# First queries in two column parts, weight chunks between the early loads, and new lengths in a planner: a fused attention and max-out kernel

## The chip, the cores and the metric

The kernel runs on one core of a Trainium2 chip. The time is device microseconds for one launch; before the change it is 384.32 us, the median of three runs (384.29 to 386.53). The profile is of one execution whose span is 382.8 us. Lines such as L436 are lines of the kernel before.

The engines are called PE (matrix multiply), ACT (scalar engine), DVE (vector engine), POOL (GpSimd) and SP (the engine that issues the DMAs here).

## The reference

There are 8 batches of 8 heads, 1152 positions and head size 64. Queries are averaged in pairs of positions, so that 576 remain; attention follows; the heads are put side by side into x (4608 tokens by 512), and a max-out layer ends it.

```python
q_pool = q.reshape(B, H, S // 2, 2, D).mean(axis=3)
scores = scale * np.matmul(q_pool, k.transpose(0, 1, 3, 2))
attn = softmax(scores)
x = (attn @ v), heads side by side           # 4608 x 512
g = np.maximum(x @ w1, x @ w2)               # 4608 x 1024
out = g @ w_out                              # 4608 x 512
```

## The kernel before, in words

**Tiling.** Work goes by pairs of heads, 32 in all, four to a batch. A pair's scores are 9 key tiles by 576 queries for each head. They are laid end to end in one row and cut into groups of 512 columns (`W`), 324 groups in all, so a pair is 10.125 groups. A group is two or more matmuls of 64 rows, both heads beside each other on the two halves of the array (L429), into one of three score buffers; one ACT instruction takes the exp of 128x1024 values (L436) into `et`. When all groups of a pair have been through exp, PE multiplies them with the values (L378), ten units of nine matmuls, and DVE divides by the row sums (L388, L390) into `xnat`.

**Before the scores.** Keys and values are cast to bf16 on POOL (L273, L304), queries are added in pairs on POOL (L297). Both are transposed, for the first five pairs on PE with a copy by DVE (L323, L349, L330, L356), later by DMA. Pair 0 is different: its two query halves, one a head and 64 partitions wide, are loaded by two DMAs (L258) and added by DVE; its keys are cast by ACT in two pieces (L279).

**The max-out layer.** It uses max(a, b) = b + max(a - b, 0). The weights come in twelve chunks: four of w2, four of w_out, four of w1. DVE casts them; `wd` is w1 - w2 (L519); w2 is transposed on PE (L531) and multiplied by w_out once into `w21` (L547, 32 matmuls of 512 columns). The work for tokens is then `h` jobs (x times `wd`, L582, and a maximum with zero, L593) and `p` jobs (x times `w21` plus the maximum times w_out, L609, twelve matmuls for 128 tokens, one copy out of PSUM by L620 or L623, and two stores by L567). It can begin when all four pairs of batch 0 are through attention and transposed into `xT`, and `wd` is there.

**The planner.** Python code writes the order out when the kernel is built. `Plan` keeps a clock for each engine and adds a `cost` in us for each operation; an engine executes its list in that order and waits on semaphores, so a wrong cost changes no result, but puts work behind a wait that the planner did not foresee. The main loop picks what PE does next: a burst of score groups if their buffers and inputs are due (`burst_now`), or a unit of one of two jobs in hand (`lane`). `burst_size` says how many groups a burst has: three if the finished batches hold over 600 tokens that the last layer has not done, else two. In the planner each change between 64-row and 128-row matmuls costs PE 0.1 us.

**Loads.** A fixed list at the end says in which order the early loads go to SP after those of pair 0, keys and queries of pair 1 and values of pair 0: k2, q2, the four w2 chunks, v1, k3, q3, the four w_out chunks, v2, k4, q4, v3, the four w1 chunks. Loads of later pairs are appended when a buffer has been read.

**The end.** The last `p` job is like the others: twelve matmuls of 512 columns, one copy by DVE, two stores issued one after the other by SP.

The lines that matter most:

```python
                    r=[f"s{r}"], w=keys + [f"s{r}"], cost=0.24 + (z - a) / 700.0)   # L438, exp
            return 3 if len(done) * SQ - p_end[0] > LAG else 2                     # L772
```

Of the kernel before, what the change touches and what calls it, by code (L numbers as in the profile page):

```python
# [15 lines left out]
class Plan:  # L16
# [38 lines left out]
    def op(self, eng, fn, r=(), w=(), dma=None, cost=0.1, mode="f", after=(), solo=False):  # L55
        n = len(self.ops)
        assert all(k in self.writer for k in r), r
        deps, raw = self.deps(r, w, after)
        prev = self.last.get(eng)
        if prev is not None and (solo or self.ops[prev]["solo"]):  # L60
            deps.add(prev)
            raw.add(prev)
        self.last[eng] = n
        t = self.when(eng, r, w, after)
        if dma is not None:
            self.free[eng] = t + (1.3 if mode == "t" else 0.5)
            self.dma_free = max(self.free[eng] + 1.2, self.dma_free) + cost
            seen = self.dma_free + 0.7
        else:
            if eng == "PE" and mode != self.mode:  # L70
                t += 0.1
                self.mode = mode
            self.free[eng] = t + cost
            seen = t + cost + self.LAT[eng]
        self.ops.append(dict(eng=eng, fn=fn, deps=deps, raw=raw, dma=dma, w=tuple(w),
                             seen=seen, end=self.free[eng], solo=solo))
        for k in r:
            self.readers.setdefault(k, set()).add(n)
        for k in w:
            self.writer[k] = n  # L80
            self.readers[k] = set()
        return n
# [71 lines left out]
def bass_funnel_attn__then__act_maxout2_kernel(  # L154
# [32 lines left out]
    with ctx:  # L187
# [10 lines left out]
        qp = [sbuf([HP, QU, 2, D], BF16, f"qp{s}") for s in range(2)]  # L198
# [31 lines left out]

        def setup():
# [21 lines left out]
        def load_q(i):  # L253
            b, h0, s = i // NHP, 2 * (i % NHP), i % 3
            for half in range(2) if i == 0 else (None,):
                at = slice(0, P) if half is None else rows(half)
                hs = slice(h0, h0 + 2) if half is None else slice(h0 + half, h0 + half + 1)
                op("SP", lambda e, at=at, hs=hs: e.dma_start(  # L258
                    qraw[s][at, :, :, :].rearrange("p u r d -> p (u r d)"),
                    q[b, hs, :, :].rearrange("h (p r) d -> (h p) (r d)", p=HP)),  # L260
                    w=["qraw0.0"] if half == 0 else [f"qraw{s}"],
                    dma="d_q" if half == 0 else f"d_q{s}", cost=1.45 if half is None else 0.75)
# [8 lines left out]
        def cast_k(i):  # L271
# [4 lines left out]
                w=[f"kbf{s}"] + (["kbf0.0", "kbf0.3"] if i == 2 else []), cost=1.13)  # L276
# [15 lines left out]

        def cast_q(i):
            s, r = i % 2, i % 3
            for half in range(2):
                a = qraw[r][rows(half), :, :, :]
                op("DVE" if i == 0 else "POOL", lambda g, half=half, a=a: g.tensor_tensor(  # L297
                    qp[s][:, :, half, :], a[:, :, 0, :], a[:, :, 1, :], ALU.add),
                    r=["qraw0.0" if i == 0 and half == 0 else f"qraw{r}"], w=[f"qp{s}.{half}"], cost=0.65 if i == 0 else 1.4,
                    solo=i > 0 and half == 1)  # L300
# [16 lines left out]
        def qtrans(i):  # L317
# [10 lines left out]
            def evac(m):  # L328
                mb = fb[m][:, :].bitcast(BF16)
                dve(lambda e: e.tensor_copy(qpT[i % 3][:, :], mb[:, 0:SQ]),  # L330
                    [f"f{m}"], [f"qpT{i % 3}", f"f{m}"], 0.4)
            return Job("q", [unit([f"qp{s}.0", f"qp{s}.1", "ident"], 0.3, go, "s")], evac, ("q", i))

# [7 lines left out]
        def ktrans_pe(i, cuts=(0, 5, 9)):  # L341
# [3 lines left out]
            for lo, hi in zip(cuts, cuts[1:]):  # L345
# [8 lines left out]
                def evac(m, lo=lo, hi=hi):  # L354
# [4 lines left out]
                        [f"f{m}"], kkeys(i, lo, hi) + [f"f{m}"], 0.1 + (hi - lo) * 0.12)  # L359
# [5 lines left out]
        def av_jobs(i):  # L365
# [5 lines left out]
            need = [f"et{es}.{g - first(i)}" for g in range(first(i), after(i))] + [f"vE{vs}", "pad"]  # L371

            def chunk(half, sb):
# [8 lines left out]
                return unit(need, 0.275, go)  # L382
# [37 lines left out]
        def skeys(g):  # L420
            return [key for i, t, *_ in pieces(g) for key in (f"kT{i % 3}.{t}", f"qpT{i % 3}")]

        def scores(g):
# [10 lines left out]
            def exp(a, z, keys):  # L434
# [3 lines left out]
                    r=[f"s{r}"], w=keys + [f"s{r}"], cost=0.24 + (z - a) / 700.0)  # L438
# [20 lines left out]
        def under(n0, n1):  # L459

            keys = [key for key, lo, hi in (("w2b", 512, 1536), ("w2T", 1536, 2560),
                                            ("w2f", 2560, NTOK)) if n0 < hi and lo < n1]
            if "w2T" in keys:
                keys += [f"w2T{ct}" for ct in range(NC_)]
            return keys
# [48 lines left out]
        def w_cast(part, ct):  # L514
            if part == 0:
                dve(lambda e: e.tensor_copy(w2b[:, ct, :], w2f[:, ct, :]),
                    [f"w2f{ct}"], [f"w2b{ct}", "w2b"], 0.6)
            elif part == 1:
                dve(lambda e: e.tensor_tensor(  # L519
                    wd[:, ct, :], w1f[:, ct, :], w2f[:, ct, :], ALU.subtract),  # L520
                    [f"w1f{ct}", f"w2f{ct}"], [f"wd{ct}", "w2f"], 1.2)
            else:
                dve(lambda e: e.tensor_copy(  # L523
                    wo[:, 2 * ct:2 * ct + 2, :], wof[:, 2 * ct:2 * ct + 2, :]),
                    [f"wof{ct}"], [f"wo{2 * ct}", f"wo{2 * ct + 1}"], 0.6)

        def w2t_job(ct):
# [7 lines left out]
            def evac(m):  # L535
# [3 lines left out]
                    [f"f{m}"], [f"w2T{ct}", "w2T", f"f{m}"], 1.15)  # L539
            return Job("w", [unit([f"w2b{ct}", "w2b", "ident"], 0.44, go)], evac)  # L540
# [19 lines left out]
        def store(lo, s):  # L560

            for half in range(2):
                n0 = lo + half * HP
                b, at = n0 // SQ, n0 % SQ
                if b % 2:
                    at = (at - NB) % SQ
                op("SP", lambda e, b=b, u=at // HP, half=half: e.dma_start(  # L567
                    out[b * SQ:(b + 1) * SQ, :].rearrange("(p u) e -> u p e", u=QU)[u, :, :],
                    osb[s][rows(half), :]), r=[f"osb{s}"], dma=f"d_o{s}", cost=0.4)
# [4 lines left out]
        def h_jobs(nb, tail):  # L574
# [4 lines left out]
            for ft in range(NF):  # L579
# [6 lines left out]
                def evac(m, ft=ft):  # L586
# [5 lines left out]
                    else:  # L592
                        dve(lambda e: e.tensor_scalar_max(  # L593
                            gT[:, ft, g0:g0 + size], fb[m][:, 0:size], 0.0),
                            [f"f{m}"], w, 0.1 + size / 960.0)
# [3 lines left out]
        def p_job(lo, tail):  # L599
            hi = lo + P  # L600

            def part(j):
                def go(e, m):
# [5 lines left out]
                    return e.matmul(fb[m][:, :], lhs, rhs, start=(j == 0), stop=(j == NC_ + NF - 1))  # L609
                if j < NC_:  # L610
                    return unit([f"w21{j}"] + xkeys(lo, hi), 0.216, go)
                return unit([f"wo{j - NC_}", f"gT.{lo % RING // P}.{j - NC_}"], 0.216, go)

            def evac(m):
                o = ocount[0] % 4
# [6 lines left out]
                else:  # L622
                    dve(lambda e: e.tensor_copy(osb[o][:, :], fb[m][:, :]),  # L623
                        [f"f{m}"], [f"osb{o}", f"f{m}"], 0.63)
                held[o] = (lo, o)
            return Job("p", [part(j) for j in range(NC_ + NF)], evac, nb=hi)
# [65 lines left out]

        def start_w(n):
            for ct in range(NC_):
                load("w", (n, ct), got_w, f"{('w2f', 'w1f', 'wof')[n]}{ct}")
# [73 lines left out]
        def burst_size():  # L769

            done = [b for b in range(B) if all(av_half.get(b * NHP + j) == 2 for j in range(NHP))]
            return 3 if len(done) * SQ - p_end[0] > LAG else 2  # L772

        def more_moe():
# [10 lines left out]
            while p_at[0] + P <= h_end[0] and f"w21{NC_ - 1}" in plan.writer:  # L785
                queue["p"].append(p_job(p_at[0], tail))
# [58 lines left out]
        def emit_unit(kk):  # L845
# [21 lines left out]
            if job.done:  # L867
# [7 lines left out]

        setup()
# [3 lines left out]
        cast_k0(0, 3, "kraw0.0")  # L880
        cast_q(0)
        cast_k0(3, NT, "kraw0")
        queue["q"].append(qtrans(0))
        queue["k"].extend(ktrans_pe(0, (0, 3, NT)))
        load_k(1)
        load_q(1)
# [6 lines left out]
        load("k", 2, load_k, "kraw2")  # L893
        load("q", 2, load_q, "qraw2")
        start_w(0)
        load("v", 1, load_v, "vraw1")
        load("k", 3, load_k, "kraw0")
        load("q", 3, load_q, "qraw0")
        start_w(2)
        load("v", 2, load_v, "vraw2")  # L900
        load("k", 4, load_k, "kraw1")
        load("q", 4, load_q, "qraw1")
        load("v", 3, load_v, "vraw0")
        start_w(1)
# [46 lines left out]
        def _(sp):  # L951
            plan.emit("SP", sp, sem, last_waits=[f"d_o{s}" for s in range(4)])
# [40 lines left out]
```

The softmax here doesn't subtract the row's maximum and nothing guards it: scores larger than these inputs give would overflow.

## Time and profile before

| what | value |
|---|---|
| time, median of 3 | 384.32 us |
| span of the profiled execution | 382.8 us |
| PE busy | 363.7 us (95%) |
| ACT busy | 316.9 us (83%), of it exp 307.8 |
| POOL busy | 162.0 us (42%) |
| DVE busy | 140.2 us (37%) |
| first score matmul; first exp | 8.27 us; 8.91 us |
| first matmul of w21; first of an h job | 43.59 us; 65.85 us |
| last copy out of PSUM begins | 378.72 us |

Busy time of PE is modelled and runs on into the next matmul, so how much PE could still do is read better from the starts of its matmuls than from its share. Shares are means over quite different stages: the first 60 us with their loads, some 270 us in which exp and matmuls go on side by side, and about 50 us at the end in which PE works alone.

### The profile page before, as it was taken

Reading aid. Unit: us, or ns where it says so; the run is one execution under the profiler, and the core shown is the slowest. Engines: PE = TensorE matmul, PEld = TensorE weight load, DVE = VectorE, ACT = ScalarE, POOL = GpSimd, SP = SyncE. Lnnn points to the kernel's source line nnn. Section 1 sums busy time; section 2 is a strip of 40 time slices with the busy share of each in tenths; the row PEclk is TensorE's granted clock in tenths of the full one; section 3 lists DMA queues with packets and bytes.
Section 4 is the critical chain, followed back from the end, with each engine's and each line's share of the span. In section 5 each row is a group of like instructions: output and inputs, shape, how many; then the busy total and the mean of one; then the engine's idle time right before and its main releaser. Section 6 shows DMA issues by size and latency. Waiting matters only on the chain.

```text
span 382.8 us, 11318 instructions
## 1 busy us (share of the span) xinstructions
PE 363.7 (95%) x5010; PEld 210.8 (55%) x5010; DVE 140.2 (37%) x283; ACT 316.9 (83%) x355; POOL 162.0 (42%) x135
## 2 busy tenths in 40 slices
PE   2787999999999999999999999999999999999995
PEld 1365546555555555455556565555455655667642
DVE  2274934442234223422252224422442244237201
ACT  3998989999999999999999999999899999902210
POOL 1955597665554555555453535545545110000000
PEclk9999999999999999999999999999999999999999
DMA  8999999999989998999799999999899460121144
GB/s 248 405 391 399 392 257 312 331 309 312 225 234 295 273 272 174 309 320 275 142 265 289 319 179 212 286 258 315 200 236 267 94 109 14 29 44 42 29 95 98
DMA packets 93521, 88.58 MB, mean 231 GB/s; under 512 B 66080, under 2 KB 66592, under 8 KB 93472
## 3 DMA queue, kind: packets, MB, share of 16 engines
q1 hardware_dynamic: 93472, 87.86, 89.4%
q8 instruction: 39, 0.64, 0.7%
q14 instruction: 10, 0.08, 0.1%
HBM read 62.91 MB, written 9.44 MB: 189 GB/s over the span
## 4 chain that ended last, share of the span: by engine, by line
PE 85%; DMA 6%; DVE 4%; POOL 2%; issue 1%; SPq 1%; POOLq 0%
PE fb L378 22%; PE fb L609 21%; PE sps L429 18%; PE fb L582 15%; PE sps L609 4%; DMA qraw<-in_q_dram 3%; DMA kraw<-in_k_dram 2%; PE sps L582 2%; DVE wd L519 2%; POOL qp L297 1%; PE fb L547 1%; DVE xnat L390 1%; POOL vE L304 1%; PE fb L489 1%; DVE wo L523 1%
## 5 line engine op out<-in xcount | busy, mean ns | idle before, releaser
L436 ACT ACTIVATE et<-sps 128x1024 bf16<-128x1024 f32 (+1 forms) x336 | 307.8, 1005 | 19.0 <-PE sps L429 17.2
L378 PEld LDWEIGHTS fb<-vE,et 128*128 128x128 bf16 x2880 | 93.4, 97 | 20.9 <-issue 10.9
L378 PE MATMUL fb<-vE,et 128*128 128x65 bf16 x2880 | 101.9, 193 | 0.3
L297 POOL TENSOR_TENSOR qp<-qraw 64x576 bf16<-64x576 f32 x62 | 88.6, 1429 | 30.6 <-DMA qpT<-qp 21.3
L429 PE MATMUL sps<-qpT,kT 64*128 64x512 bf16 (+7 forms) x1152 | 96.9, 289 | 3.0 <-ACT et L436 2.1
L304 POOL TENSOR_SCALAR vE<-vraw 128x1152 bf16<-128x1152 f32 x32 | 36.9, 1152 | 103.2 <-PE fb L378 95.8
L429 PEld LDWEIGHTS sps<-qpT,kT 64*128 64x128 bf16 x1152 | 41.8, 95 | 51.3 <-issue 19.6
L582 PE MATMUL fb<-xT,wd 128*128 128x512 bf16 (+3 forms) x276 | 63.1, 360 | 0.7 <-DVE stage L623 0.7
L609 PE MATMUL fb<-wo,stage 128*128 128x512 bf16 x240 | 62.4, 380 | 0.0
L593 DVE TENSOR_SCALAR stage<-fb 128x512 bf16<-128x512 f32 (+3 forms) x64 | 41.9, 657 | 32.3 <-PE fb L582 32.1
L388 DVE RECIPROCAL rc<-fb 128x5 f32<-128x5 f32 x64 | 12.4, 194 | 112.3 <-PE fb L378 112.3
L273 POOL TENSOR_SCALAR kbf<-kraw 128x1152 bf16<-128x1152 f32 x31 | 36.2, 1167 | 14.6 <-DMA kraw<-in_k_dram 12.5
L582 PEld LDWEIGHTS fb<-xT,wd 128*128 128x128 bf16 x276 | 22.8, 98 | 29.4 <-DVE stage L593 6.3
L623 DVE COPY stage<-fb 128x512 f32<-128x512 f32 x29 | 20.0, 690 | 50.2 <-PE fb L609 49.7
L609 PEld LDWEIGHTS fb<-wo,stage 128*128 128x128 bf16 x240 | 21.1, 97 | 23.3 <-issue 3.3
L390 DVE TENSOR_TENSOR xnat<-fb,rc 128x320 bf16<-128x320 f32 x64 | 31.5, 491 | 2.2
L609 PE MATMUL fb<-w,xT 128*128 128x512 bf16 x120 | 32.1, 380 | 0.0
L609 PEld LDWEIGHTS fb<-w,xT 128*128 128x128 bf16 x120 | 10.3, 98 | 11.7 <-issue 2.0
L589 ACT ACTIVATE stage<-sps 128x256 bf16<-128x256 f32 (+1 forms) x7 | 2.3, 338 | 16.4 <-PE sps L582 16.4
L620 ACT COPY stage<-sps 128x512 f32<-128x512 f32 x3 | 1.8, 585 | 13.8 <-PE sps L609 13.8
L609 PE MATMUL sps<-wo,stage 128*128 128x512 bf16 x48 | 11.3, 379 | 0.0
L582 PE MATMUL sps<-xT,wd 128*128 128x256 bf16 (+2 forms) x76 | 10.3, 275 | 0.0
(40 smaller groups left out, 96.4 us busy)
## 6 DMA issues: line engine op xcount, KB each, us to landing
vraw<-in_v_dram SPq DMA_DIRECT2D x32, 576.0 KB, 7.7
kraw<-in_k_dram SPq DMA_DIRECT2D x31, 576.0 KB, 6.6
qraw<-in_q_dram SPq DMA_DIRECT2D x31, 576.0 KB, 5.8
out_dram<-stage SPq DMA_DIRECT2D x72, 128.0 KB, 2.4
xT<-in_moe_w_dram SPq DMA_DIRECT2D x4, 512.0 KB, 11.9
stage<-in_moe_w_out_dram SPq DMA_DIRECT2D x4, 512.0 KB, 14.2
stage<-in_moe_w_dram SPq DMA_DIRECT2D x4, 512.0 KB, 13.2
qraw<-in_q_dram SPq DMA_DIRECT2D x2, 288.0 KB, 4.1
```

The lines of the kernel that those rows point to most:

```text
L273: op("POOL", lambda g: g.tensor_scalar(kbf[s][:, :, :, :].rearrange("p t h d -> p h t d"), kraw[r][:, :, :, :], 1.0, 1.0, ALU.mult, ALU.mu ...
L297: op("DVE" if i == 0 else "POOL", lambda g, half=half, a=a: g.tensor_tensor(qp[s][:, :, half, :], a[:, :, 0, :], a[:, :, 1, :], ALU.add), ...
L304: op("POOL", lambda g: g.tensor_scalar(vE[r][:, :, :, 0:D].rearrange("p t h d -> p h t d"), vraw[r][:, :, :, :], 1.0, 1.0, ALU.mult, ALU.m ...
L378: last = e.matmul(fb[m][:, sb * 66:sb * 66 + 65], et[:, a:a + P], vE[vs][:, t, half, 0:65], start=(t == 0), stop=(t == NT - 1))
L388: dve(lambda e: e.reciprocal(rc[half][:, :], a[:, :, 64:65]), [f"f{m}"], [f"rc{half}"], 0.19)
L390: dve(lambda e: e.tensor_tensor(xnat[xs][:, :, c:c + D], a[:, :, 0:D], rc[half][:, :].unsqueeze(2).to_broadcast([P, NCH + 1, D]), ALU.mult ...
L429: last = e.matmul(sps[r][:, h, col:col + hi - lo], kT[i % 3][rows(h), t, :], qpT[i % 3][rows(h), lo:hi], start=True, stop=True)
L436: op("ACT", lambda e: e.activation(et2[:, :, c:c + z - a], sps[r][:, :, a - g * W:z - g * W], EXP, scale=scale), r=[f"s{r}"], w=keys + [f" ...
L582: return e.matmul(fb[m][:, 0:size], wd[:, ct, ft * P:(ft + 1) * P], xT[:, ct, n0:n1], start=(ct == 0), stop=(ct == NC_ - 1))
L593: dve(lambda e: e.tensor_scalar_max(gT[:, ft, g0:g0 + size], fb[m][:, 0:size], 0.0), [f"f{m}"], w, 0.1 + size / 960.0)
L609: return e.matmul(fb[m][:, :], lhs, rhs, start=(j == 0), stop=(j == NC_ + NF - 1))
L623: dve(lambda e: e.tensor_copy(osb[o][:, :], fb[m][:, :]), [f"f{m}"], [f"osb{o}", f"f{m}"], 0.63)
```

## The change

It has five parts.

1. **The first queries.** The pair-0 load is cut by columns (five and four of nine) and not by heads, so each part covers all 128 partitions. DVE adds each part on 128 partitions (`cast_q0`), and PE transposes it in 64x64 blocks (`qtrans0`). The first keys are cast, transposed and copied in three pieces (1, 2 and 6 tiles), not two (3 and 6), so that the first score group can begin with one key tile.
2. **The order of early loads.** q1 goes ahead of k1; the weight chunks (a: w2, b: w_out, c: w1) are spread singly between the loads of queries, keys and values.
3. **The planner's lengths.** exp goes from 0.24 + n/700 to 0.05 + n/600 (0.971 to 0.903 us for a full group); DVE copies and maxima get 0.16 us in place of 0.1 or so; the first DMA starts at 0.78 us, not at 0. `burst_size` gives three as soon as any batch is finished.
4. **Waits.** Weight keys are kept by chunk, so a transpose of one w2 chunk no longer waits for the cast of a later one. The last value unit of a pair, which reads 64 columns past its own scores, now names the neighbour's first group as an input.
5. **The last tile.** It is two jobs, 384 and 128 columns. ACT empties the first while PE does the second; DVE empties the second, whose stores go out from SP and ACT, one each.

```diff
+            if not self.dma_free:
+                t = 0.78
...
+        Q0 = (0, 5, QU)
...
-            for half in range(2) if i == 0 else (None,):
+            for lo, hi in zip(Q0, Q0[1:]) if i == 0 else ((0, QU),):
...
+        def cast_q0(j):
+            lo, hi = Q0[j:j + 2]
+            op("DVE", lambda e: e.tensor_tensor(
+                q0[:, lo:hi, :], qraw[0][:, lo:hi, 0, :], qraw[0][:, lo:hi, 1, :], ALU.add),
+                r=["qraw0" if j else "qraw0.0"], w=[f"qp0.{j}"], cost=0.1 + (hi - lo) * 0.07)
...
+                past = [f"et{1 - es}.0"] if sb == NCH and not es & half else []
+                return unit(need + past, 0.275, go)
...
-                    r=[f"s{r}"], w=keys + [f"s{r}"], cost=0.24 + (z - a) / 700.0)
+                    r=[f"s{r}"], w=keys + [f"s{r}"], cost=0.05 + (z - a) / 600.0)
...
-            return Job("w", [unit([f"w2b{ct}", "w2b", "ident"], 0.44, go)], evac)
+            return Job("w", [unit([f"w2b{ct}", "ident"], 0.44, go)], evac)
...
+                if c0 == 0:
+                    op("ACT", lambda e: e.copy(osb[o][:, c0:c1], fb[m][:, 0:c1 - c0]),
+                       r=[f"f{m}"], w=[f"osb{o}", f"f{m}"], cost=0.16 + (c1 - c0) / 1200.0)
+                    store(lo, o, c0, c1)
+                else:
+                    dve(lambda e: e.tensor_copy(osb[o][:, c0:c1], fb[m][:, 0:c1 - c0]),
+                        [f"f{m}"], [f"osb{o}", f"f{m}"], 0.16 + (c1 - c0) / 960.0)
+                    store(lo, o, c0, c1, ("SP", "ACT"))
...
-            return 3 if len(done) * SQ - p_end[0] > LAG else 2
+            return 3 if done else 2
...
-                queue["p"].append(p_job(p_at[0], tail))
+                if p_at[0] + P < NTOK:
+                    queue["p"].append(p_job(p_at[0], tail))
+                else:
+                    queue["p"].extend(p_job(p_at[0], tail, *c) for c in ((0, 384), (384, E)))
...
+        K0 = (0, 1, 3, NT)
...
+        for lo, hi in zip(K0, K0[1:]):
+            cast_k0(lo, hi, "kraw0.0" if hi <= 3 else "kraw0")
+        queue["k"].extend(ktrans_pe(0, K0))
+        load_q(1)
         load_k(1)
-        load_q(1)
...
-        start_w(1)
+        whole = {"q": load_q, "k": load_k, "v": load_v}
+        part = {"a": (0, "w2f"), "b": (2, "wof"), "c": (1, "w1f")}
+        for kind, i in zip(*[iter("q2a0a2k2a1a3b1b0b2v1b3c0v2k3q3k4q4c2c1v3c3")] * 2):
```

## The prediction

> **What bounds the kernel.** I read the page's slices first, then the stages.
>
> ```profile
> PE   2787999999999999999999999999999999999995
> ACT  3998989999999999999999999999899999902210
> ...
> DMA  8999999999989998999799999999899460121144
> ```
>
> A slice is 9.57 us. PE is full from the fifth slice to the end, ACT until 332 us only, DMA is full at the start. So from 40 us on the kernel ends when PE's list ends; ACT has some 47 us to spare. Only four things can move the end: PE's idle time before it is full, PE's own overhead later, waits that a new order brings, and what follows the last matmul.
>
> ```profile
> 0.00:8.00 8.00, 1.09 (x12) 0.74 (x12) 2.09 (x4) 2.35 (x3) 0.97 (x10) 1.00 0.76 217
> 8.00:12.00 4.00, 3.62 (x28) 1.86 (x29) 0.77 (x2) 3.39 (x5) 2.36 (x2) 1.00 1.04 400
> ...
> 20.00:30.00 10.00, 8.95 (x180) 6.67 (x179) 7.57 (x14) 9.97 (x13) 5.16 (x4) 1.00 1.05 391
> 30.00:40.00 10.00, 7.48 (x159) 5.08 (x157) 4.51 (x10) 8.96 (x11) 6.25 (x5) 1.00 1.04 402
> 40.00:60.00 20.00, 18.94 (x280) 10.63 (x276) 12.89 (x20) 18.95 (x22) 15.85 (x11) 1.00 1.13 321
> 60.00:80.00 20.00, 19.92 (x307) 11.57 (x306) 8.97 (x19) 19.82 (x23) 13.88 (x12) 1.00 1.13 314
> ```
>
> The third number is PE's busy time. Idle is 6.91 in the first 8 us, 2.44 from 8 to 20 (the rows left out give 0.90 and 1.16), and 1.05 + 2.52 + 1.06 = 4.63 from 20 to 60. Then 0.08.
>
> ```profile
> PE fb L323 <- DVE qp L297: 6.7, 1, 6.7
> PE sps L429 <- ACT et L436: 2.1, 5, 0.5
> PE fb L349 <- POOL kbf L273: 1.5, 1, 1.5
> ```
>
> PE's waits (total, count, longest): the start hangs on the first queries. PE hardly waits for exp. The 1.5 us is at 35.25: the transpose of k4, whose load landed at 33.98 by its semaphore, blocks PE, and ACT stands 1.03 us.
>
> **What the Trainium skill says.** SBUF — State Buffer, section Door 1: partitions 0 to 63 reach 8 of the 16 DMA ports, 196 GB/s against 328 for 128 partitions at 1 MiB. The trace agrees: in slices of 1.5 us the DMAs moved
>
> ```profile
> GB/s 0 123 258 259 377 415 398 393 407 410 412 407 400 394 406 385 387 392 382 388 394 413 386 405 406 410 397 413 392 392 404 319 129 356 392 438 203 108 229 369
> ```
>
> 258 while the query halves were on their way, some 400 later. TensorEngine Tiling, Key Properties: a change of tiling mode drains the array; the trace prices it below. DMA: Bandwidth & Descriptors, "Issuing engines are not separate DMA queues": a second issuing engine saves only issue time; no run here shows two yet.
>
> **Part 1, start.** DVE gets the first half at 4.61 and the second at 5.91 (starts of its adds), the key pieces land at 6.42 and 7.44. ACT casts 7.46 to 8.30, the first exp is at 8.91. The queries' 590 KB at 390 GB/s take 1.5 us; from 2.0, where packets begin, to 4.5 they took 2.5. I let all later landings come 1.0 us earlier, up to 1.4 if the slow first packets go too: keys at 5.4 and 6.4. The adds are 0.75 for 576 elements; with 1.04 ns an element (DVE copies of 128 and 512 columns: 0.29 and 0.69) they are 0.48 and 0.42, hidden before the keys. The 18 blocks are no longer than the 9 transposes (0.66) by more than 0.3, also before the keys. One key tile then goes through cast 0.31, transpose 0.2, copy 0.23 and gaps in 1.2 us, against 1.85 for three, so the first score would be at 6.6. But ACT has the cast of six tiles (0.84) in its list before the first exp: 6.4 + 0.84 + 0.1 = 7.35. Gain 8.91 - 7.4 = **1.5 us** (0.8 to 1.8). Exp paces the next 20 us, so all moves with it.
>
> **Part 2, load order.** A 576 KB load takes 1.45 us, a chunk 1.31 (differences of landings: 9.30, 10.72, 12.24; 15.18 to 21.80 for four chunks and v1). From keys at 6.4 the new list lands: q1 7.9, k1 9.3, v0 10.8, q2 12.2, w2 chunks 13.6 to 18.9, w_out chunks 20.2 to 25.6 (before: about 26.9 to 31), v1 24.3, c0 26.9, v2 28.4, k3 29.8, q3 31.3, k4 32.7, q4 34.2, last w1 chunk 39.5 (42.1). The product w21 needs all of w2 and w_out: possible from 27.5, before it began at 43.59:
>
> ```profile
> 43.59 1.25 PE L547 MATMUL fb<-wo,xT 128*128 128x512 bf16 x5
> ...
> 65.85 1.03 PE L582 MATMUL fb<-xT,wd 128*128 128x512 bf16 x4
> ```
>
> It is 32 x 0.216 = 6.9 us of PE work, in exactly the stretch where PE idles 4.6 us. Before, it came after that stretch, held both lanes, and delayed the value products of pair 3 (exp done at about 46, last unit at 57.8) and with it the first h job. Balance: a pair costs PE 10.1 groups at 0.31 with switches, 90 value matmuls at 29.5 ns (2.65) and 1.1 of transposes, 6.9 in the 9.27 us that exp takes. From 27.5 the w21 work fills the rest until about 48, then x of batch 0 is ready at some 52 and h begins at 52 to 57. Idle from 20 to 60 falls from 4.6 to 0.8: **3.8 us** (1.5 to 4.6). Queued behind the late k3 and q3: q3 lands at 31.3, POOL adds for 2.9, transpose and copy 1.1, ready at 35.3; pair 3 needs it at 7.4 + 30.4 x 0.92 = 35.4. A near miss; that is the 0.8 I leave. If it is late, the scores queued on PE stand, and exp behind them.
>
> **Part 3, lengths and bursts.** Back-to-back exps start 0.903 us apart in the trace, which is what the new formula says; the old 0.971 was long. So bursts come no earlier than the buffers do; I add no wait. Switches:
>
> ```profile
> 94.25 1.51 PE fb L609 x7
> 96.52 2.27 PE fb L609 x10
> 98.79 0.76 PE sps L429 x12
> ```
>
> In the chain, seven matmuls take 7 x 0.216 = 1.51; ten after a switch 2.27 - 2.16 = 0.11 more; three groups 0.76 - 0.65 = 0.11 more. Start to start it is 0.095 each way, 0.19 a burst. Counting runs of L429 after 60 us: 107 bursts for 271 groups, 65 of three groups, 36 of two. All in threes would be 91: 16 x 0.19 = 3.0. Some twos come from inputs and not from the rule; I take 11: **2.1 us** (0.5 to 3.0). Longer bursts let ACT stand a little; it has 47 us.
>
> **Part 4, waits.** Dropped chunk waits: in the shadow of DVE's lazy casts, 0. The new input of the last value unit: seven pairs in eight share that group with the next pair and wait for it anyway; behind it queue the unit's lane and a later exp. 0 to 0.3 in all.
>
> **Part 5, end.** Last matmul ends 378.70, copy 0.69, SP issues at 379.44 and 379.95, landed 382.33. After: 12 x (162 + 56) ns is as long as 12 x 216. The 128-column copy takes 0.29 (row above), saving 0.40. But SP first issues two stores of the 384 part: ACT's copy 0.585 - 128 x 0.83 = 0.48 ends 0.2 before the last matmul, so SP is free 1.0 after it; its third issue starts 0.25 earlier than the last one before, with a quarter of the bytes. **0.4 us** (0.1 to 0.8).
>
> Sum: 1.5 + 3.8 + 2.1 + 0.4 = 7.8, less 0.1 for part 4: 384.3 - 7.7 = 376.6.
>
> **Rivals.**
> - *The loads take it back.* q3 and v2 come 6 us later than before (q3 landed at 25.5). If DMA runs 1 to 2 us behind my table, PE stands behind pair 3 as it did behind k4, and idle from 20 to 60 stays at 4 us. For: the 0.1 us margin. Against: w21 can be put before it. 1.5 + 0.6 + 1.0 + 0.3: 380.9.
> - *PE waits for exp.* With an exact exp length every burst is due at the last moment, and any lag makes PE stand with h and p work queued behind it. Before, the slack was 3 x 0.07 a burst and waits were 2.1 us. At 0.1 for 110 bursts that is 11 us, against gains of 7.7: 387.6, slower. Against: PE's value units are planned at 0.275 and take 0.266, so PE, too, has little lead, and the pitch is exact.
> - *All of it.* Bursts all of three, no idle after 20, start 1.8: 1.8 + 4.6 + 3.0 + 0.8 = 10.2: 374.1 or a little under.
>
> **Numbers.** Mine 0.62, all of it 0.14, loads 0.15, PE waits 0.09. The range 373 to 381.5 holds the first two and most of the third. Below 380.5 are the first two and a few of the third: 0.78; within 1% 0.14; slower 0.08.
>
> **What would show it.** First exp near 7.4; L547 from about 28 and L582 from 52 to 57; PE idle from 20 to 60 under 1.5; L429 runs after 60 us near 96; PE waiting for L436 still around 2 us; SP's last issue 1.0 after the last matmul. I am wrong if PE's waits for exp pass 5 us, if ACT stands over 2 us near 35, or if h begins no earlier.

## The result and the profile after

The changed kernel takes 390.64 us, the median of four runs (388.70 to 392.97), against 384.81 us for the kernel before, also the median of four: ratio 1.0147, 95% interval 1.0102 to 1.0192. It was to be faster by 2%, and is slower by 1.5%. The profiled execution, the fastest of the four, has a span of 386.9 us, against 382.8. The time lies some 1.8 us above the span in every run.

The slices of the page, PE and ACT:

```profile
PE   3898989999999999999999999999999999999994
ACT  3998989999999999999999999999999985111121
```

PE is as full as before, to the end. ACT's row falls off one to two slices earlier: exp is done at 324.0 us, 11.1 before its old end, and PE does not end earlier for it. The stages that the prediction costed, with the same columns (the third number is PE's busy time):

```profile
0.00:8.00 8.00, 2.10 (x23) 0.97 (x23) 1.96 (x6) 2.24 (x4) 0.97 (x10) 1.00 0.74 252
8.00:12.00 4.00, 2.88 (x24) 1.34 (x26) 0.56 (x1) 3.46 (x5) 1.37 (x2) 1.00 1.02 405
...
20.00:30.00 10.00, 9.06 (x194) 6.79 (x192) 6.17 (x12) 9.93 (x13) 1.48 (x3) 1.00 1.05 393
30.00:40.00 10.00, 8.36 (x155) 5.58 (x150) 7.03 (x14) 8.94 (x11) 9.49 (x7) 1.00 1.03 403
40.00:60.00 20.00, 17.41 (x271) 9.79 (x268) 13.27 (x16) 18.63 (x22) 18.54 (x13) 1.00 1.07 310
60.00:80.00 20.00, 19.97 (x301) 11.79 (x300) 9.39 (x20) 18.95 (x23) 12.13 (x10) 1.00 1.15 293
```

Idle from 20 to 60 us is 0.94 + 1.64 + 2.59 = 5.2 us; it was 4.6 and was to be 0.8. From 40 to 60 it rose from 1.06 to 2.59. POOL is fuller there (18.54 for 15.85). In the first 12 us PE works 4.98 us, before 4.71. So the start gave next to nothing, and the middle cost.

What follows after 60 us is not seen in busy shares: 19.97 of 20. It is seen in the chain of work that ended last. First the page of the kernel before, then of the changed one (shares of the span by engine):

```profile
PE 85%; DMA 6%; DVE 4%; POOL 2%; issue 1%; SPq 1%; POOLq 0%
```

```profile
PE 83%; ACT 8%; DVE 6%; DMA 1%; issue 0%; SPq 0%
```

ACT was not on the chain at all, and now holds 8% of it. Followed near the end of exp, the chain of the changed kernel reads (start, length, what):

```profile
288.94 4.70 ACT et L469 x5
293.64 0.05 issue
293.69 0.39 PE sps L462 x4
...
298.28 5.40 ACT et L469 x6
303.68 0.02 issue
303.70 2.22 ACT et L469 x3
305.93 0.05 issue
305.97 0.39 PE sps L462 x4
```

Five, six and three exps in a row set the end, and then PE's next group follows 0.05 us after the exp that gave its buffer back. The same from ACT's side, its waits for scores (us in total, times, longest), before and after:

```profile
ACT et L436 <- PE sps L429: 17.2, 57, 1.0
```

```profile
ACT et L469 <- PE sps L462: 6.7, 12, 1.1
```

ACT used to stand 57 times, now 12 times: PE stands instead. Taking each start of a matmul inside a burst after 60 us against the pitch of a running PE, PE stands 4.0 us in the changed kernel, most of it in some 25 pieces of about 0.13 us, and 0.25 us before. These pieces are too short for the list of PE's waits, which has about 2 us for exp in both kernels.

At the end, the last matmul ends at 381.4 us (378.7 before), and 5.5 us follow (4.15 before).

**A ledger.** The list is the order that the planner wrote out, with its own clock: the costs that it adds up while the kernel is built. By this clock PE would end at 379.3 us for the list of before, at 376.5 for the changed one. The lag is the start of an exp in the trace less its start on the list: how far the chip is behind the list there. The last column is the median of the runs; the others come from the one profiled execution, which for the changed kernel lies 1.9 us under its median.

| kernel | list: PE ends | lag at 55 us | lag of the last exp | last matmul ends | PE stands in bursts | time |
|---|---|---|---|---|---|---|
| before | 379.3 | 2.3 | -0.9 | 378.7 | 0.25 | 384.7 |
| changed | 376.5 | 4.0 | 4.7 | 381.4 | 4.0 | 390.6 |
| e1 | 376.5 | 5.0 | 5.7 | 382.4 | 4.2 | 388.3 |
| e3 | 376.2 | 4.3 | 5.7 | 382.1 | 5.7 | 388.2 |
| e5 | 376.5 | 5.3 | 2.1 | 378.8 | 0.3 | 384.4 |
| e8 | 373.8 | 3.0 | 2.9 | 377.1 | 0.9 | 381.2 |
| e9 | 377.3 | 5.9 | 4.8 | 382.3 | 2.2 | 388.4 |
| e10 | 378.0 | 5.4 | 3.4 | 381.7 | 2.2 | 388.1 |
| e11 | 378.7 | 1.4 | -1.0 | 378.0 | 1.0 | 385.0 |
| e13 | 375.7 | 2.5 | 5.5 | 381.5 | 7.0 | 388.9 |
| e15 | 373.8 | 2.2 | 0.4 | 374.5 | 1.0 | 379.9 |

From before to changed: the list is 2.85 us shorter, the lag at 55 us is 1.7 larger, and between there and the end it rises by 0.7 where it fell by 3.1, so 3.8 more. -2.85 + 1.7 + 3.8 = 2.7, which is 381.4 - 378.7. With 1.3 more after the last matmul it is 4.0 of the 4.1 us between the spans. The ledger thus speaks of this execution, and not of the 1.9 us up to the median.

The fall by 3.1 in the kernel before comes from the exps. Its list holds 2.6 us of waits inside bursts, for exps that it takes to be longer than they are, and the chip stood 0.25 there. Matched one by one with the list from 55 us to the last scores, the steps from one group to the next inside a burst took 37.7 us where the list has 39.4 before the change, and 41.8 where it has 39.1 after it. That is a swing of 4.4 us, and PE's own lag, which fell by 3.6 before and rose by 0.7 after, swings by 4.3: the bursts are all of it. Value units are not the source: start to start they take 0.275 us before and 0.274 after, and the list has 0.275. The experiments are about the three terms.

### The profile page after: what moved, and what is told of

Its sections match the earlier page's. It is cut to its first block, busy times and chain, and to the rows that moved or that the text cites. A ratio compares the mean times of both kernels' runs of the same rounds, so it can differ in the third digit from the quotient of the medians.

```text
span 386.9 us, 11368 instructions
## 1 busy us (share of the span) xinstructions
PE 367.4 (95%) x5031; PEld 212.2 (55%) x5031; DVE 139.5 (36%) x279; ACT 318.7 (82%) x363; POOL 165.4 (43%) x135
## 4 chain that ended last, share of the span: by engine, by line
PE 83%; ACT 8%; DVE 6%; DMA 1%; issue 0%; SPq 0%
PE fb L409 21%; PE fb L643 19%; PE sps L462 19%; PE fb L616 12%; ACT et L469 7%; PE sps L643 5%; PE sps L616 3%; DVE wd L551 2%; DMA kraw<-in_k_dram 1%; DVE xnat L422 1%; PE fb L579 1%; DVE wo L555 1%; PE fb L379 1%; PE sps L409 1%; PE fb L563 1%; PE fb L521 1%
## 5 line engine op out<-in xcount | busy, mean ns | idle before, releaser
L462 PE MATMUL sps<-qpT,kT 64*128 64x512 bf16 (+7 forms) x1152 | 100.9, 292 | 4.2 <-ACT et L469 2.1
L409 PEld LDWEIGHTS fb<-vE,et 128*128 128x128 bf16 x2790 | 89.5, 97 | 16.5 <-issue 9.2
L409 PE MATMUL fb<-vE,et 128*128 128x65 bf16 x2790 | 96.3, 193 | 2.0 <-DVE w L584 1.1
L315 POOL TENSOR_SCALAR vE<-vraw 128x1152 bf16<-128x1152 f32 x32 | 38.9, 1217 | 63.5 <-PE fb L409 53.0
L616 PE MATMUL fb<-xT,wd 128*128 128x512 bf16 (+3 forms) x264 | 61.0, 355 | 0.1
L643 PE MATMUL fb<-wo,stage 128*128 128x512 bf16 x224 | 57.5, 380 | 0.0
L627 DVE TENSOR_SCALAR stage<-fb 128x512 bf16<-128x512 f32 (+3 forms) x57 | 37.4, 657 | 24.9 <-PE fb L616 24.4
L616 PEld LDWEIGHTS fb<-xT,wd 128*128 128x128 bf16 x264 | 22.8, 98 | 23.8 <-issue 5.1
L623 ACT ACTIVATE stage<-fb 128x256 bf16<-128x256 f32 (+2 forms) x9 | 3.6, 396 | 18.1 <-PE fb L616 18.1
L643 PE MATMUL sps<-wo,stage 128*128 128x512 bf16 (+2 forms) x72 | 15.3, 355 | 0.0
L616 PE MATMUL sps<-xT,wd 128*128 128x256 bf16 (+3 forms) x88 | 14.2, 299 | 0.0
```

Source lines behind the costliest of these rows:

```text
L315: op("POOL", lambda g: g.tensor_scalar(vE[r][:, :, :, 0:D].rearrange("p t h d -> p h t d"), vraw[r][:, :, :, :], 1.0, 1.0, ALU.mult, ALU.m ...
L409: last = e.matmul(fb[m][:, sb * 66:sb * 66 + 65], et[:, a:a + P], vE[vs][:, t, half, 0:65], start=(t == 0), stop=(t == NT - 1))
L462: last = e.matmul(sps[r][:, h, col:col + hi - lo], kT[i % 3][rows(h), t, :], qpT[i % 3][rows(h), lo:hi], start=True, stop=True)
L616: return e.matmul(fb[m][:, 0:size], wd[:, ct, ft * P:(ft + 1) * P], xT[:, ct, n0:n1], start=(ct == 0), stop=(ct == NC_ - 1))
L627: dve(lambda e: e.tensor_scalar_max(gT[:, ft, g0:g0 + size], fb[m][:, 0:size], 0.0), [f"f{m}"], w, 0.16 + size / 960.0)
L643: return e.matmul(fb[m][:, 0:c1 - c0], lhs, rhs[:, c0:c1], start=(j == 0), stop=(j == NC_ + NF - 1))
```

## The experiments

Theory A: without slack in the exp length the list is tighter than the chip, PE stands inside bursts, and no delay is made up. Rivals: the late rise of PE's clock (C), the new order of loads, the longer bursts. All kernels from e5 on have one more condition in the planner's main loop, so that both parts of the last tile are always listed.

**e1, the end.** The stores of the tile before the last are sent before the last tile's own.

```diff
                 if c0 == 0:
+                    for x in list(held):
+                        store(*held.pop(x))
                     op("ACT", lambda e: e.copy(osb[o][:, c0:c1], fb[m][:, 0:c1 - c0]),
```

> The changed kernel, with one thing moved: the stores of the last tile but one are put ahead of those of the last tile. The order of every compute engine is the same. Theory (stores of the last tile but one, ready 2 us before the end, stand behind the last tile's in SP's list): from the last matmul to the end of the span 4.1 us in place of 5.5, the time 1.4 us (1.0 to 1.8) under the changed kernel's. Rival (the split itself costs the time, by its small rows and third and fourth store): no more than 0.5 us under it.

388.27 us (387.78 to 388.89), ratio to before 1.009 (1.0063 to 1.0117). The tail falls from 5.47 to 3.70 us, by 1.8; between the medians it is 2.4, for which the spread of the changed kernel (388.70 to 392.97) leaves room. In the changed kernel the stores of a tile wait in `held` until 2 us have passed on the plan, their buffer is wanted again, or the plan is over. ACT had copied the last tile but one at 379.42 us; its two stores were issued at 383.30 and 383.94, behind those of the last tile. The changed kernel's stores from 376 us on:

```profile
L600 SPq DMA_DIRECT2D out_dram<-stage x7: 466/597/815, 377.0 to 383.9; - x7
L600 ACTq DMA_DIRECT2D out_dram<-stage x1: 568/568/568, 381.8 to 381.8; - x1
```

SP's last issue starts 2.5 us after the last matmul; in e1 it starts at 383.5, 1.1 us after. That is what the prediction reckoned for its part 5. From e5 on, all kernels built on the changed one have this mended.

**e2, the old lengths.** Changed kernel with the planner's old lengths, old burst rule and old last tile.

```diff
-                    r=[f"s{r}"], w=keys + [f"s{r}"], cost=0.05 + (z - a) / 600.0)
+                    r=[f"s{r}"], w=keys + [f"s{r}"], cost=0.24 + (z - a) / 700.0)
...
-            return 3 if done else 2
+            return 3 if len(done) * SQ - p_end[0] > LAG else 2
```

> The changed kernel with the planner's old lengths (exp 0.24 + n/700, DVE lengths, first DMA at 0), the old rule for bursts and the last tile as before; the start, the load order and the waits as changed. Theory A (exact exp lengths take the slack out of the order, so delays before 60 us are kept and PE stands inside bursts of scores): exp stands more than 12 us in all between 60 and 320 us, PE loses under 1 us inside bursts (4.0 in the changed kernel), and the time falls back to 381 to 385.5. Rival B (the new start and load order cost the time, by a clock that comes late and by late loads): it stays at 387 to 391.

389.26 us (388.58 to 389.41), in the range of the rival. Between exps ACT stood 26.8 us from 60 to 320 us (27.3 before the change, 17.4 after it), so the slack was back; but this list happens to hold one burst of seven groups, planned to stand 3.9 us, and it did for 3.5. Its list ends at 381.8 of itself. It tells nothing between the theories; it shows that each edit makes a new list, whose own length moves by some us.

**e3, the exp length alone,** on the kernel before.

```diff
-                    r=[f"s{r}"], w=keys + [f"s{r}"], cost=0.24 + (z - a) / 700.0)
+                    r=[f"s{r}"], w=keys + [f"s{r}"], cost=0.05 + (z - a) / 600.0)
```

> The kernel before with the new exp length alone (0.05 + n/600). Theory A: the planner now packs exp without slack, the 2 us that the start runs late are not caught up, PE loses 2 to 4 us inside bursts (0.3 before), and the time is 383 to 387, no better than before although the planner's own clock ends 3 us earlier. Rival B (lengths are harmless, the new start and loads do the damage): the time falls by the planner's 3 us, to 380 to 382.5.

388.21 us (388.11 to 390.32), ratio 1.0101 (1.0065 to 1.0137): 3.8 us slower by one number, and worse than either side expected. The list is 3.1 us shorter and the last matmul 3.4 later. PE stands 5.7 us inside bursts, and the page's chain reads

```profile
PE 76%; ACT 19%; DMA 2%; DVE 1%; SPq 1%; issue 0%; POOL 0%
```

Beside the tail (1.8 us in e1's trace) this is of the size of the whole difference of 5.8. The lag does not grow in the same places, though. In e3 it rises in small steps, from 2.3 us at 10 us to 4.3 at 55 and 5.0 at 100. In the changed kernel it is still 2.0 at 45 us, and rises by 1.9 in the ten us after that, where something else acts too (see e7).

**e4, PE's clock.** Twenty-six transposes of the identity ahead of all else.

```diff
+            for _ in range(26):
+                last = e.transpose(mb[:, 0:P], ident[:, :], ident[:, :])
```

> The changed kernel with 26 transposes of the identity put ahead of PE's first work, while PE waits for the first queries (work that is not needed). Theory C (in the changed kernel PE gets its full clock 6 us later than before, at 20.7 against 14.4 us, and in some executions later still, which costs 1 to 4 us and spreads its times over 388.7 to 393): full clock by 8 us, times within 1 us of each other and 2 to 4 us under the changed kernel's median. Theory A alone: the time within 1 us of the changed kernel's, since exp paces that stretch and not PE.

389.48 us (388.44 to 389.89). The clock was full from 5.0 to 8.5 us, then half again until 22.1: it did not stay, so the run says little of C. See e6.

**e5, real slack.** e1, each exp 32 columns a head shorter, the list unchanged. It leaves a part of the softmax out: these columns are set to zero once, at the start (not shown).

```diff
-                    et2[:, :, c:c + z - a], sps[r][:, :, a - g * W:z - g * W], EXP, scale=scale),
-                    r=[f"s{r}"], w=keys + [f"s{r}"], cost=0.05 + (z - a) / 600.0)
+                    et2[:, :, c:c + z - a - 32], sps[r][:, :, a - g * W:z - g * W - 32], EXP, scale=scale),
+                    r=[f"s{r}", "pad"], w=keys + [f"s{r}"], cost=0.05 + (z - a) / 600.0)
```

> The kernel of e1 with every exp instruction 32 columns a head shorter (the last 32 columns of each piece are left at zero, so part of the softmax is left out); the order on every engine is exactly that of e1, and the planner still counts 0.903 us. By 0.83 ns for each of 64 elements an exp is 0.053 us shorter. Theory A (PE loses time because exp has no slack in this order): loss inside bursts after 60 us falls from 4.2 to under 1, exp stands more, and the time falls by 3 to 5 us from e1's 388.3, to 383.3 to 385.3. Rival (exp does not pace PE after 60 us; the losses lie before it): at most 1 us less.

384.36 us (382.71 to 388.10, 19 runs), ratio 0.9998 (0.9979 to 1.0017), 3.9 us less than e1. An exp takes 0.05 us less, PE stands 0.3 us in bursts instead of 4.2, and from the same lag at 55 us (5.3) the chip makes up 3.2. Same order, same loads, same bursts of three: so none of these by itself keeps the lag. What keeps it is that exp has no slack in this list, as A says. ACT waits for scores again as in the kernel before:

```profile
ACT et L470 <- PE sps L463: 19.7, 54, 2.5
```

**e6, the clock again.** e1 with early score matmuls issued twice, which keeps PE busy.

```diff
-                for i, t, lo, hi, col in pieces(g):
+                for i, t, lo, hi, col in list(pieces(g)) * (2 if 1 <= g < 14 else 1):
```

> The kernel of e1 with the score matmuls of groups 1 to 13 issued twice into the same buffer (work that is not needed), so that PE is busier from 9 to 22 us; the order is otherwise that of e1. Theory C (the full clock comes late, at 23 us in e1, because PE is too little used, and that costs time): full clock by 14 us, PE's work is then 1 to 3 us ahead and the time 386 to 387. Rival: the clock comes early and the time stays within 0.7 us of 388.3, since exp sets the pace there and PE has time over.

387.89 us (387.31 to 388.67), 0.4 less than e1, and within the spread of both. The clock is full from 12.5 us (22.9 in e1), and PE loses 3.3 us less between 12 and 22 us; yet the lag at 55 us is 4.9, as in e1. C alone does not explain the time.

**e7, casts not held back.** e1, with the lazy casts let go whenever DVE is free on the plan.

```diff
-            if lazy and plan.free.get("DVE", 0.0) <= now() and not any(
-                    queue[kind] and ready_at(queue[kind][0]) <= now() + 1.5 for kind in "qk") and all(
-                    j is None or j.kind not in "qk" for j in lane.values()):
+            if lazy and plan.free.get("DVE", 0.0) <= now():
```

> The kernel of e1 without the rule that holds back casts of weights while a query or key transpose is due (the cast goes as soon as DVE is free). Theory (in the changed kernel the early chunks bring nothing because this rule keeps the last w_out cast until 44.8 us): the first matmul of w21 comes at 26 to 33 us in place of 46, the first h job at 60 to 64, PE's loss from 30 to 60 us falls by 3 or more. If this stretch is worth what the prediction said, the time falls by 3 to 4 us; if it is given back later in bursts that wait for exp, by 1 or less.

387.31 us (386.39 to 390.28, 11 runs), 1.0 less than e1; the two ranges overlap. w21 begins at 34.5 us for 46.7 and h at 64.9 for 69.8, and no lag is added at 55 us; but 1.7 us came at 20 us, where the clock rose only at 23.8.

What happens at 55 us is in the chain of the changed kernel:

```profile
44.86 1.23 DVE wo L555
46.08 4.16 DVE wd L551 x2
50.25 0.60 DVE w L584
50.85 3.56 DVE wd L551 x2
...
54.55 0.50 DVE xnat L422
55.05 0.05 issue
55.10 1.55 PE fb L409 x45
```

For ten us DVE alone sets the pace: the last w_out cast, held until then, and the four subtracts. The subtract is planned at 1.4 us. Its rows (busy, mean ns) in the kernel before, the changed one, and e8 below:

```profile
L519 DVE TENSOR_TENSOR wd<-stage,xT 128x1024 bf16<-128x1024 f32 x4 | 6.3, 1595 | 0.0
```

```profile
L551 DVE TENSOR_TENSOR wd<-stage,xT 128x1024 bf16<-128x1024 f32 x4 | 7.9, 2010 | 0.0
```

```profile
L551 DVE TENSOR_TENSOR wd<-stage,xT 128x1024 bf16<-128x1024 f32 x4 | 4.9, 1235 | 0.7 <-DMA stage<-in_moe_w_dram 0.7
```

The Trainium skill, SBUF — State Buffer, section "Who interferes with whom", says that a DVE instruction with two SBUF inputs contends with a GpSimd instruction that reads SBUF. The trace agrees: the first two subtracts (4.24 us) lie beside two value casts of POOL, from 47.06 on, which took 4.20 instead of twice 1.16. Four subtracts at 2.01 and a cast at 1.31 are 3.1 us over the list.

**e8, slack, casts let go, old order.** e7 with 0.04 us of slack in the exp length, the old burst rule and the old load order.

```diff
-                    r=[f"s{r}"], w=keys + [f"s{r}"], cost=0.05 + (z - a) / 600.0)
+                    r=[f"s{r}"], w=keys + [f"s{r}"], cost=0.090 + (z - a) / 600.0)
...
-            return 3 if done else 2
+            return 3 if len(done) * SQ - p_end[0] > LAG else 2
...
-        for kind, i in zip(*[iter("q2a0a2k2a1a3b1b0b2v1b3c0v2k3q3k4q4c2c1v3c3")] * 2):
+        for kind, i in zip(*[iter("k2q2a0a1a2a3v1k3q3b0b1b2b3v2k4q4v3c0c1c2c3")] * 2):
```

> The kernel of e7 with the exp length 0.943 us (0.09 + n/600, 0.04 more than measured), the old rule for bursts and the old order of chunks. Theory A: the slack lets exp catch up what the start loses, loss inside bursts stays under 1.5, and the time is 377 to 381, under both kernels. Rival (the order is chance, any change of lengths reshuffles it): 384 to 389.

381.20 us (379.95 to 382.46), ratio 0.9894 (0.9855 to 0.9933): faster than both kernels. Its list ends at 373.8 us; the lag stays near 3.

**e9 and e10, slack in the list alone.** e1 with 0.07 (e9) and 0.08 (e10) for 0.05 in the exp length.

```diff
-                    r=[f"s{r}"], w=keys + [f"s{r}"], cost=0.05 + (z - a) / 600.0)
+                    r=[f"s{r}"], w=keys + [f"s{r}"], cost=0.070 + (z - a) / 600.0)
```

> e1 with one number changed: the planner takes an exp at 0.923 us (0.07 + n/600) instead of 0.903, 0.02 us of slack on each. Load order, start, burst rule, last tile as in e1. Theory A (no slack, so no delay is caught up): 271 times 0.02 is 5.4 us, so the 4 us by which the exps lag at 54 us are caught up, but only after some 200 exps: PE's standing inside bursts falls from 4.2 to 2 to 3, exps' lag ends near zero, the time is 385.5 to 387.5. Rival (the new load order, or bursts of three as such, cost the time): standing stays near 4 and the time at 387.5 to 389.5.

> As e9 with 0.933 us (0.08 + n/600), 0.03 us of slack. Theory A: the lag is gone after some 130 exps, and PE's standing inside bursts is 1 to 2.5, of which some 2 is in the plan itself; this plan ends 0.8 us later than that of e9, so the gain over e1 is partly paid for: 385 to 387.5. Rival: standing near 4, 388 to 390.

388.37 us (386.99 to 389.36) and 388.09 us (386.47 to 389.84). The standing halves to 2.2 us, as A has it, and from 55 us on the lag falls by 1.1 and 1.9 where in e1 it rose by 0.7. But the lists are 0.8 and 1.5 us longer, and the time is e1's, in the rival's range both times. Slack on the plan is paid for on the plan, which the expectation of e10 named in part and neither priced in full. Real slack (e5) is not. So A is right on the mechanism, and the exp length is no knob by itself; it pays where the list is short for other reasons, as in e8.

**e11, the new loads again.** e8 with the changed kernel's load order.

```diff
-        for kind, i in zip(*[iter("k2q2a0a1a2a3v1k3q3b0b1b2b3v2k4q4v3c0c1c2c3")] * 2):
+        for kind, i in zip(*[iter("q2a0a2k2a1a3b1b0b2v1b3c0v2k3q3k4q4c2c1v3c3")] * 2):
```

> e8 (slack of 0.04, old burst rule, casts not held back, old load order; 381.2) with only the changed kernel's load order put back. If the load order is neutral once there is slack: 380 to 382.5. If it costs (query and key loads of pairs 3 and 4 come 6 us later, so PE and exp stand between 20 and 60 us, and the planner's own list is 4.9 us longer): 384 to 387, with PE's standing inside bursts still under 2 us.

385.01 us (383.37 to 387.12, 20 runs): 3.8 us slower than e8. h began earlier than in e8 (60.3 us for 63.9), and the chip kept to the list (lag 1.4, then -1.0); the list itself is 4.9 us longer. With this planner the new order does not pay.

**e12, e8 with the new burst rule** and half the slack.

```diff
-                    r=[f"s{r}"], w=keys + [f"s{r}"], cost=0.090 + (z - a) / 600.0)
+                    r=[f"s{r}"], w=keys + [f"s{r}"], cost=0.070 + (z - a) / 600.0)
...
-            return 3 if len(done) * SQ - p_end[0] > LAG else 2
+            return 3 if done else 2
```

> e8 with a smaller slack (0.02 instead of 0.04) and the changed kernel's burst rule (three once a batch is ready): fewer bursts, some 104 after 60 us in place of 107, and a planned end 0.9 us earlier. If 0.02 is slack enough: 379.5 to 382. If it isn't, PE stands inside bursts for 2.5 to 4 us again and the time is 382.5 to 385.

386.28 us (383.09 to 387.29, 12 runs), outside what was expected on either side. The list is the shortest of all (372.9), and the lag 3.2 us until 100 us, where one wait adds 5.2:

```profile
PE fb L616 <- DMA xT<-xnat: 3.7, 1, 3.7
```

```profile
105.00:108.00 3.00, 0.78 (x4) 0.32 (x4) 0.00 (x0) 0.96 (x2) 0.00 (x0) 0.96 0.86 159
108.00:112.00 4.00, 4.00 (x19) 1.20 (x19) 1.39 (x2) 1.02 (x1) 3.38 (x3) 0.60 0.96 221
```

PE has an h job next in its list, whose x is still in the DMA transposes (SP issues them from 97.6 us on, and the last lands at 107.1). Behind it stand the scores. Then the clock (the number before the last two) is at 0.60 for 4 us. The Trainium skill, TensorE: Matmul & The Clock Gate, section "What's actually happening", says that the clock falls to half after an idle window of about 3.4 us; an idle of 3.65 us did it here. A whole window of idle is not needed by what e5 shows: there it fell to half at 39.4 us with no idle over 1.65 us in the ten us before.

**e13, both hindrances away.** e7 with e6's edit.

> e7 (casts not held back) with the score matmuls of groups 1 to 13 issued twice, as in e6, so that PE's clock is up early. Where the lag behind the plan comes from is read off the exps: in e7 1.6 us came at 20 us, where PE's clock rose at 23.8, and none at 54; in e6 the reverse, none at 20 and 2.1 at 54. Theory D (two hindrances side by side, a slow clock at 20 us and the subtracts of DVE at 54, each of which hides the other): without both the exps lag by about 2.4 us at 60 us instead of 4.5 to 4.9, and the last matmul ends near 379: 384.5 to 386. Rival (a third thing fixes the lag near 4.7): 387 to 388.5.

The lag at 55 us is 2.5, as Theory D had it (e6 4.9, e7 4.4): in these three traces late clock and DVE's chain stand side by side and each hides the other. The time is 388.92 us (386.46 to 391.50), outside the ranges of the theory and of its rival. The lag stays at 2.6 to 3.2 until 271 us, where a group of scores waits 2.2 us, and jumps to 5.3. The profile puts that wait down to an exp; the exp that freed this buffer had ended 2.8 us earlier, so it was another input: the keys of the next pair, whose first scores are in this group. SP issued their DMA transpose at 268.8, it landed at 273.28, and the group starts at 273.34.

**e14, the last tile alone,** on the kernel before, with the held stores first (e1's edit and part 5 of the change).

> The kernel before with the last tile alone changed: two parts, ACT and DVE, two issuing engines, and the held stores sent first as in e1. Everything ahead is the same list. Prediction's part 5 with its omission mended: tail after the last matmul 3.7 us instead of 4.15, 384.0 to 384.4 (0.2 to 0.6 less than before). Rival: the end is set by the stores' own flight, no gain: 384.4 to 385.

384.17 us (383.37 to 386.74, 20 runs) beside 384.67: ratio 0.9993 (0.9978 to 1.0008). The tail is 3.68 us for 4.15. The shorter tail is of the size that part 5 claimed; the times alone don't tell it from no gain.

**e15, e8 with e6's edit.**

> e8 with the score matmuls of groups 1 to 13 issued twice. In e8's profile the clock was up at 14.9 us by itself, so little is left to win there; if other executions had it later, their median falls: 380 to 381.2. If the clock doesn't matter or the second scores cost PE time that exp waits for: 381.2 to 382.5.

379.91 us (379.45 to 380.25), ratio 0.9873 (0.9847 to 0.9898): the lowest median of all, though its interval and that of e8 overlap. Its stages, to be compared with the rows above:

```profile
20.00:30.00 10.00, 9.95 (x199) 7.35 (x197) 7.78 (x15) 9.94 (x12) 5.16 (x4) 1.00 1.05 391
30.00:40.00 10.00, 10.00 (x153) 5.99 (x153) 7.54 (x13) 10.00 (x13) 6.53 (x5) 1.00 1.04 402
40.00:60.00 20.00, 19.71 (x350) 12.46 (x348) 11.62 (x23) 19.97 (x24) 13.97 (x11) 1.00 1.12 305
```

Idle from 20 to 60 us is 0.05 + 0 + 0.29, with the old order of loads (a few doubled scores fall into the first row). The lag falls to 0.4, so the short list is kept. So little idle was possible in this stretch, though not by the means of the change.

## Why the prediction was wrong, by its own steps

**Part 3, where it failed most.** "So bursts come no earlier than the buffers do; I add no wait." Each burst comes when the buffers would be free if ACT had kept to the list. ACT starts 1.5 us late and never gets ahead, because a full exp now has no slack. So PE, which cannot pass over a group, stands in the burst: 4.0 us (e3: 5.7). The rival "PE waits for exp" was this, with its chance of 0.09 and a size of 11 us that came out at 4. It was put aside in part on a reading that is wrong: a value unit does not take 0.266 us, nine times the usual pitch of its matmuls, but 0.274 to 0.275 from start to start, just what the list says. The lead of the kernel before lay in its exps, planned at 0.971 us and done in 0.903, and the new length took it away. The saving was counted too high as well: 261 changes of mode became 251, 10 x 0.095 = 0.95 us, not 2.1. Runs of scores after 60 us fell from 107 to 100.

**Part 2.** "Possible from 27.5" left out what stands between load and product. The last w_out chunk landed at 27.2 us, for 25.6 in the table; w21 began at 46.0, as the cast of that chunk ran at 44.77. The first h job began at 68.8 us, where 52 to 57 was hoped for and 65.85 was the time before, so one of the named signs of being wrong came true. The planner holds casts back while query or key work is due or in hand, and the keys and queries of pairs 3 and 4 now come late, in just this stretch. I had read the loads and not the rule that lets the casts go. Without that rule w21 begins at 34.5 us (e7) and 32.4 (e13), so 27.5 was too early in any case. The subtracts then fell beside POOL's casts and took 2.01 us for a planned 1.4. Idle from 20 to 60 us became 5.2, not 0.8. The DMAs ran some 1.5 us behind the table (q3 landed at 32.87 for 31.3), as in the rival "the loads take it back", but ACT stood only 1.06 us for it, at 38 us.

**Part 1.** The queries did land earlier (3.67 and 4.49 us for 4.59 and 5.89), but the key pieces at 5.57 and 7.63 (6.40 and 7.44), against the 5.4 and 6.4 reckoned. "I let all later landings come 1.0 us earlier" is the step that failed: the next two loads were both in at 10.55, before at 10.72. The first score came at 6.63, as reckoned; but ACT's cast of the second key piece, ahead of the first exp in its list, could begin only at 7.66. So the first exp, reckoned at 7.4, is at 8.40, and then

```profile
8.40 1.01 ACT L469 ACTIVATE et<-sps 128x1024 bf16<-128x1024 f32 x1
8.55 0.82 PE L379 MATMUL fb<-ident,kbf 128*128 128x128 bf16 x6 [0.99 <-ACT kbf L284]
9.31 1.46 PE L462 MATMUL sps<-qpT,kT 64*128 64x64 bf16 x12
...
9.96 2.86 ACT L469 ACTIVATE et<-sps 128x1024 bf16<-128x1024 f32 x3 [0.55 <-PE sps L462]
```

the second must wait until six key tiles are cast, transposed and copied. Over the 14 profiles with the new start the first exp is at 8.35 us in the mean and the third at 10.88; over the three with the old start (before, e3, e14) at 8.77 and 10.59. By the third exp the gain is gone, where 1.5 us was to stay.

**Part 4** shows no cost in PE's list of waits, which has no value unit that waits for an exp; no run has this part alone. **Part 5** was right on the operations (e14), and missed one: the stores held back. Instead of 0.4 gained, 1.3 lost, 1.8 against e1.

The same counted at PE, as idle time beyond the pitch of a running PE: start 9.48 us before and 9.52 after (to 12 us), 12 to 60 us 9.5 and 11.9, later 3.9 and 5.7, changes of mode 0.95 less. That is 3.3 us of loss for the 2.7 by which the last matmul moved; 0.6 of it is not accounted for. The prediction summed stages, each as though the rest would move up by itself; in a list written out beforehand a gain has to be planned and then kept.

What stays open: why some lists are 2 to 5 us shorter than others (e8 against e11), which is the planner's own choice and was not taken apart; and how much of a median is due to PE's clock, which differs from execution to execution: over the 20 of e11 a lower granted clock goes with a longer time (correlation -0.85), over 20 of e14 it does not (0.08).

## What to carry to other kernels

A planned length has two jobs, to tell the truth and to leave room: before you make it exact, look whether a wait with other work queued behind it now hangs on it, and compare plan and trace as a lag over time, not as a sum. When data come earlier, look for the rule that issues their consumer, since that may be what sets its start. When the last piece of work is split, list what else is still queued ahead of or behind it on the issuing engine.

## What the runs showed of the hardware

- Two loads of 64 partitions one after the other cost the loads behind them little. The next two loads were both in at 10.80 us in the mean of the three profiles with such halves, and at 10.53 in the mean of the 14 with parts of 128 partitions. In the two slices of 1.5 us in which the DMAs moved 258 and 259 GB/s before the change, they moved 286 and 319 after it, and some 400 later in both: most of what was missing at 258 was not due to the halves.
- PE's clock was full for good from a time between 12.5 and 24.5 us, by kernel and execution. Only two profiles have it at half again later: e12 after the idle of 3.65 us, and e5, where PE idled 2.8 of the ten us before 40, from 39.4 to 42.8. Profiles with full clock by 15.5 us add at most 0.2 us of lag between the 13th and the 19th exp, those later than 20 us between 0.1 and 1.7 (2.0 a little earlier in e2).
- A 128x1024 subtract on DVE took 1.2 us by itself and 2.0 in the mean beside POOL; POOL's casts went from 1.16 to 2.1.
- A score group that waits for the exp that frees its buffer starts 0.055 us after that exp's end.
